# The leaky activation as a maximum, and an earlier start of w_out2's conversion

## The chip, the cores and the metric

One core of one Trainium2 chip. The metric is the device time of one execution in microseconds (us); the kernel before was run three times.

## The reference

Retention attention with a decay per head feeds two gated networks, one behind the other:

```python
ret = scores * Dmat                 # causal, decay gamma ** (i - j), per head
x = (ret @ v)                       # 2304 tokens x 512
y = ((x @ w1) * (x @ w2)) @ w3 @ w_out            # 512 -> 1024 -> 512
h = y @ moe2_w_in                                  # 512 -> 2048
g = np.maximum(h, 0.0) + alpha * np.minimum(h, 0.0)   # alpha: one per column, rand() * 0.3
out = g @ moe2_w_out                               # 2048 -> 512
```

q, k, v, alpha and the result are float32; the weights arrive as float64 and are turned into float32 on the chip.

## The kernel before, in words

Everything is in feature-major tiles of 128 partitions. Every large product runs three times on TensorE (PE), over a high and a low part of each operand: high by high, high by low, low by high. The order on PE, on ScalarE (ACT) and on SyncE (SP, the only queue that issues DMAs) is the order of the code. VectorE (DVE) is ordered by the scheduler; a built program has one fixed order for it too. Semaphores make each engine wait where an operand isn't there.

The stages are attention (to 70 us), a and b and their product (to 279 us), w3 times w_out (to 323 us), y (to 422 us), the **g stage** and the **out stage**. The change touches the last two, and a few tiny instructions early in the attention.

**g stage** (class Group, L871 to L935, loop at L970). The 2304 tokens are three pairs p of blocks of 384 (W), the 2048 columns of h are eight groups j of 256 (m is its half). For one (p, j) a Winograd scheme makes h from seven products of six matmuls, of 384 columns each, 42 in all: p1, p5, p6, p2 of this group and, in between, p7, p4, p3 of the group before (its order on PE is p1, p5, p7 before, p6, p2, p4 before, p3 before). PSUM banks b1, b2, b3 hold the sums. p1 is followed by an ACT copy of b1 to b2 (L909), on which p6 adds; p5 and p6 by ACT copies of their sums into SBUF tiles p5 and u2 (L914, L919). Two of the four tiles of h are ready in PSUM after p2 and p4, and from_psum makes g of them: two Relu on ACT (L894, L895), one scalar_tensor_tensor on DVE (L896). The other two are the sum of a bank and of p5 or u2, after p7 and p3, and from_sum takes three DVE instructions each (L902, L903, L904). p4 writes the bank that p7's from_sum reads, so PE waits for L902. g goes to DRAM (keep, L867) from six SBUF buffers.

**w_out2's conversion** (class Weights, L57 to L136). 16 tiles of 128 x 512 float64 go through four steps: raw is loaded by SP (three buffers); `_first` is two ACT instructions (L93, L94); `_second` four on DVE (L103, L104, L106, L108); `_third` an ACT cast to the high part (L112); `_fourth` a DVE subtraction for the low part (L116). One `tick` does each step once, for pieces one apart, in the order fourth, third, second, first. So the cast of a piece stands on ACT ahead of what the program does next, and waits for L108 of that piece. In pair p = 2, one tick follows each group j from 2 on; the first out steps do the rest.

**out stage** (L1030). 48 steps (j, b): blocks 0 and 1 are done together, j by j, then the others. A step loads g back (load_g, into gr, three buffers), splits it (split_g, one step ahead: an ACT cast to gh, L172, a DVE subtraction to gl, L173) and runs 18 matmuls of 512 columns on three banks. The first matmuls of a step need gh, the third needs gl. The first three load_g are in groups j = 5, 6, 7 of p = 2, split_g(0) in j = 7.

`al` holds alpha in its first 16 columns, and its negative in the next 16 (L863, one DVE instruction that the scheduler puts at 20 us).

Of the kernel before, what the change touches and what calls it, by code (L numbers as in the profile page):

```python
# [11 lines left out]
AF = mybir.ActivationFunctionType  # L12
ALU = mybir.AluOpType
# [11 lines left out]
C2 = DF2 // P  # L25
# [7 lines left out]
def _f32(ap):  # L33
    return ap.bitcast(F32)
# [24 lines left out]
class Weights:  # L59
# [14 lines left out]
        self.pieces, self.raw, self.ab, self.dest = [], {}, {}, {}  # L74
        self.loaded, self.at = 0, [0] * 4

    def add(self, src, dest):

        self.pieces.append((src, dest))

    def load_until(self, n):
        while self.loaded < min(n, len(self.pieces)):
# [26 lines left out]

    def _third(self, i):  # L110
        self.dest[i] = self.pieces[i][1]()
        self.nc.scalar.copy(self.dest[i][0], self.ab[i][0])  # L112

    def _fourth(self, i):
        hi, lo = self.dest.pop(i)
        self.nc.vector.tensor_tensor(out=lo, in0=self.ab.pop(i)[0], in1=_f32(hi), op=ALU.subtract)  # L116

    def tick(self, upto=None):

# [18 lines left out]
def retention_moe_kernel(ctx: ExitStack, tc, qk, kv, w_out1, w3t, w12, w_in, w_out2, alpha, c_row, c_pair, out):  # L138
# [11 lines left out]


    al = const.tile([P, 96], F32, name="al")
    al, neg = al[:, 0:C2], al[:, C2:2 * C2]
    const_r = pool(ctx, "const_r", side="right")
    const_r.tile([P, 120], F32, name="pad")

# [35 lines left out]
    def goes_to(table, key, make):  # L192
        def dest():
            t = make()
            table[key] = t[:, 0], t[:, 1]
            return table[key]
        return dest
# [654 lines left out]
    def wb_tile(c):  # L852
        if c < 8:
            return in_wa(C1 + c, f"wb{c}")
        if c < 14:
            return hold.tile([P, 2, DM], F32R, tag=f"wu{c}", name=f"wb{c}")
        return in_wa(c - 14, f"wb{c}")

    n_in = len(ws.pieces)
    for c in range(C2):  # L860
        ws.add(w_out2[c], goes_to(wbc, c, lambda c=c: wb_tile(c)))

    nc.vector.tensor_scalar(out=neg, in0=al, scalar1=-1.0, scalar2=None, op0=ALU.mult)  # L863

    gd = {}

# [4 lines left out]
    class Group:  # L871
# [16 lines left out]
        def tile(self, tag, bufs=2):  # L888
            return gp.tile([P, W], F32, tag=tag, name=f"{tag}{self.n}", bufs=bufs)

        def from_psum(self, ps, m, t):
            c = 2 * self.j + m
            r, g = self.tile("m"), self.tile("g", 6)
            nc.scalar.activation(r, ps, AF.Relu, scale=-1.0)  # L894
            nc.scalar.activation(g, ps, AF.Relu)  # L895
            nc.vector.scalar_tensor_tensor(out=g, in0=r, scalar=neg[:, c:c + 1], in1=g, op0=ALU.mult, op1=ALU.add)  # L896
            keep(c, 2 * self.p + t, g)

        def from_sum(self, a, b, m, t):
            c = 2 * self.j + m  # L900
            r, g = self.tile("m"), self.tile("g", 6)
            nc.vector.tensor_tensor(out=g, in0=a, in1=b, op=ALU.add)  # L902
            nc.vector.tensor_scalar(out=r, in0=g, scalar1=0.0, scalar2=al[:, c:c + 1], op0=ALU.min, op1=ALU.mult)  # L903
            nc.vector.scalar_tensor_tensor(out=g, in0=g, scalar=0.0, in1=r, op0=ALU.max, op1=ALU.add)  # L904
            keep(c, 2 * self.p + t, g)

        def p1(self):
            self.product(self.b1, "A11", "B11")
# [1 line left out]

        def p5(self):
            self.product(self.b3, "S1", "T1")
            self.p5s = self.tile("p5")
            nc.scalar.copy(self.p5s, self.b3)  # L914

        def p6(self):
            self.product(self.b2, "S2", "T2", False)
            self.u2 = self.tile("u2")
            nc.scalar.copy(self.u2, self.b2)  # L919

        def p2(self):
            self.product(self.b1, "A12", "B21", False)
# [47 lines left out]
    for n, (p, j) in enumerate(groups):  # L970
        last, first = j == C1 - 1 and p + 1 < NP, j == 0 and p > 0
        g = Group(p, j, n)
        flush()
        g.p1()
        g.p5()
        if last:
            some_of(make, 1)
        if before:
            before.p7()
        flush()  # L980
        if first:
            some_of(make, 2)
        g.p6()
        if last:
            some_of(make, 1)
        g.p2()
        if last:
            some_of(make, 1)
        flush()
        if before:  # L990
            before.p4()
            if first:
                some_of(make, 2)
                if p + 1 < NP:
                    x_room(p + 1)
                    for o in range(KT):
                        for t in range(2):
                            nc.sync.dma_start(out=xs_of[p + 1][:, o, t], in_=x2d[2 * (p + 1) + t, o])
                else:
                    pt.close()  # L1000
                    gr = pool(ctx, "gr", side="left", bufs=3, reuse_waits="tile")
                    ghl = pool(ctx, "ghl", side="left", bufs=2, reuse_waits="tile")
            before.p3()
        if j == 5 and p + 1 < NP:
            make = x_operands(p + 1)
        if j in (5, 6):
            some_of(make, 1)
        if p == 0:
            some_of(fetches, 4)
        if p == NP - 1:  # L1010
            if j == 0:
                ws.load_until(n_in + 3)
            if j >= 2:
                ws.tick()
            if j >= 5:
                load_g(j - 5)
            if j == 7:
                split_g(0)
        before = g
# [10 lines left out]
    for n, (j, b) in enumerate(steps):  # L1030
        if ws.at[3] < len(ws.pieces):
            ws.tick()
            ws.until(n_in + 2 * j + 2)
        load_g(n + 3)
        split_g(n + 1)
        if b not in accs:
            accs[b] = [bank((used + i) % 8, f"o{b}_{i}") for i in range(NM)]
# [92 lines left out]
```

## Time and profile before

| | us |
|---|---|
| median of three runs (lowest to highest) | 803.81 (803.64 to 804.98) |
| the profiled execution: span | 801.9 |
| PE busy in it | 787.0 (98%) |
| DVE busy in it | 498.6 (62%) |
| ACT busy in it | 348.9 (44%) |
| g stage, first to last matmul | 422.3 to 599.9 |
| out stage, first to last matmul | 599.9 to 798.4 |

The page gives the profiled execution's span alone, 1.9 us below the median of the runs; what lies around the span isn't on it. Times of rows are counted from the span's start. A row of the timeline has the start, the length of one instruction (or of a group, from its first start to its last end), the engine, the line and operation, out<-in, the shape and the count; in brackets the engine's idle time before it, and who ended it. Instructions of an engine overlap a little, so the distance from start to start (the pitch) is what one costs its engine, and its length is what the next engine waits for. PE's clock stands at its full level in every stretch of the g and out stages.

### The profile page before, as it was taken

What the parts mean: (1) busy time and instruction counts of PE and PEld (TensorE: products, weight loads), DVE (VectorE), ACT (ScalarE), POOL (GpSimd) and SP (SyncE); (2) the same over time, 40 slices, a digit from 0 to 9 for tenths busy, and PEclk for the clock granted to TensorE, in tenths of its full rate; (3) what the DMA queues carried; (4) which work ended last, traced back from release to release, by engine and by line L of the source; (5) the groups of instructions that cost most, each with busy time, mean ns of one, the idle gap of its engine ahead of it and who ended that gap; (6) DMA issues with size and microseconds to landing.
All of it is one profiled execution on the core that took longest, in us unless ns stands there. A gap on an engine that the chain in (4) does not pass through costs nothing.

```text
span 801.9 us, 12688 instructions
## 1 busy us (share of the span) xinstructions
PE 787.0 (98%) x4768; PEld 694.4 (87%) x4768; DVE 498.6 (62%) x895; ACT 348.9 (44%) x648; POOL 0.2 (0%) x4
## 2 busy tenths in 40 slices
PE   7899999999999999999999999999999999999998
PEld 4678888888888988999999999999987888888886
DVE  4895785325477799888833677587899923222232
ACT  3453562231255566656514465465666522222121
POOL 0000000000000000000000000000000000000000
PEclk8999999999999999999999999999999999999999
DMA  9843931561366669899916925225557635344341
GB/s 347 343 159 120 345 150 54 166 247 54 116 201 181 201 201 353 285 400 407 381 46 216 358 100 197 109 98 199 184 194 247 209 99 177 106 132 138 99 136 42
DMA packets 81341, 156.24 MB, mean 195 GB/s; under 512 B 9600, under 2 KB 57728, under 8 KB 81280
## 3 DMA queue, kind: packets, MB, share of 16 engines
q1 hardware_dynamic: 81280, 155.43, 55.6%
q8 instruction: 37, 0.61, 0.3%
q14 instruction: 24, 0.20, 0.1%
HBM read 104.02 MB, written 51.38 MB: 194 GB/s over the span
## 4 chain that ended last, share of the span: by engine, by line
PE 90%; DVE 4%; DMA 2%; issue 1%; ACT 1%; SPq 1%; ACTq 0%; DVEq 0%
PE ps L179 25%; PE o L1045 23%; PE h L884 18%; PE y L817 12%; PE pw L631 5%; PE sc L287 2%; PE o L342 2%; PE o L333 1%; PE st L302 1%; DMA kv<-in_kv_dram 1%; DMA xs<-x2d 1%; DMA gr<-gd 0%; DVE gl L173 0%; DVE g L902 0%; DVE g L896 0%
## 5 line engine op out<-in xcount | busy, mean ns | idle before, releaser
L179 PE MATMUL ps<-xh,w 128*128 128x512 f32 (+1 forms) x640 | 186.0, 372 | 0.6 <-DVE w L116 0.3
L1045 PE MATMUL o<-wb,gh 128*128 128x512 f32 x576 | 177.6, 389 | 1.1 <-ACT gh L172 1.1
L179 PEld LDWEIGHTS ps<-xh,w 128*128 128x128 f32 x640 | 116.0, 188 | 22.3 <-DVE w L116 0.7
L1045 PEld LDWEIGHTS o<-wb,gh 128*128 128x128 f32 x576 | 108.1, 188 | 23.8 <-ACT gh L172 1.5
L179 PE MATMUL ps<-xl,w 128*128 128x512 f32 (+1 forms) x320 | 118.0, 369 | 0.0
L1045 PE MATMUL o<-wb,gl 128*128 128x512 f32 x288 | 112.3, 390 | 0.4 <-DVE gl L173 0.4
L173 DVE TENSOR_TENSOR gl<-gr,gh 128x768 fp32r<-128x768 f32 x48 | 45.9, 957 | 100.1 <-ACT gh L172 100.1
L817 PE MATMUL y<-yab,wp 128*128 128x384 f32 x576 | 100.0, 334 | 0.0
L817 PEld LDWEIGHTS y<-yab,wp 128*128 128x128 f32 x576 | 99.9, 188 | 0.1
L172 ACT CAST gh<-gr 128x768 fp32r<-128x768 f32 x48 | 40.2, 838 | 116.5 <-PE o L1045 112.0
L179 PEld LDWEIGHTS ps<-xl,w 128*128 128x128 f32 x320 | 60.4, 189 | 9.8 <-DVE xl L173 0.3
L1045 PEld LDWEIGHTS o<-wb,gl 128*128 128x128 f32 x288 | 54.1, 188 | 12.5 <-DVE gl L173 1.3
L896 DVE SCALAR_TENSOR_TENSOR g<-m,al,g 128x384 f32<-128x384 f32 x48 | 29.7, 618 | 49.3 <-ACT g L895 47.8
L884 PE MATMUL h<-xT,wv 128*128 128x384 f32 x288 | 54.9, 334 | 1.5 <-DVE g L902 1.5
L884 PE MATMUL h<-xT,wu 128*128 128x384 f32 x288 | 55.0, 335 | 0.5 <-ACT h L909 0.3
L884 PEld LDWEIGHTS h<-xT,wv 128*128 128x128 f32 x288 | 50.3, 188 | 1.8 <-DVE g L902 1.8
L108 DVE CUSTOM_DVE_ANT_0 a<-a,b 128x1024 uint16<-128x1024 uint16 x72 | 49.5, 688 | 3.3
L884 PEld LDWEIGHTS h<-xT,wu 128*128 128x128 f32 x288 | 50.2, 188 | 1.1 <-ACT h L909 0.6
L488 ACT CAST ab<-f 128x512 fp32r<-128x512 f32 (+1 forms) x40 | 23.1, 577 | 63.8 <-DVE f L492 59.4
L492 DVE TENSOR_TENSOR f<-f,ps 128x512 f32<-128x512 f32 (+1 forms) x40 | 25.3, 632 | 30.8 <-PE ps L179 30.6
L103 DVE TENSOR_SCALAR a<-a 128x512 f32<-128x512 f32 x72 | 30.4, 422 | 22.3 <-ACT a L93 21.9
L631 PE MATMUL pw<-wo,w 128*128 128x512 f32 x192 | 43.7, 389 | 0.0
(95 smaller groups left out, 1008.8 us busy)
## 6 DMA issues: line engine op xcount, KB each, us to landing
gd<-g SPq DMA_DIRECT2D x96, 192.0 KB, 1.9
gr<-gd SPq DMA_DIRECT2D x96, 192.0 KB, 2.6
abd<-ab SPq DMA_DIRECT2D x32, 512.0 KB, 4.1
raw<-in_w_out_dram SPq DMA_DIRECT2D x24, 512.0 KB, 3.9
yab<-abd SPq DMA_DIRECT2D x24, 384.0 KB, 8.2
raw<-in_w_dram SPq DMA_DIRECT2D x16, 512.0 KB, 6.9
raw<-in_w3t_dram SPq DMA_DIRECT2D x16, 512.0 KB, 4.1
rawi<-in_w_in_dram SPq DMA_DIRECT2D x16, 512.0 KB, 6.1
```

Source lines behind the costliest of these rows:

```text
L103: nc.vector.tensor_scalar(out=a, in0=a, scalar1=self.LEAST, scalar2=self.MOST, op0=ALU.max, op1=ALU.min)
L108: nc.vector.tensor_tensor(out=a.bitcast(I32), in0=a.bitcast(I32), in1=b, op=ALU.add)
L172: nc.scalar.copy(hi, src)
L173: nc.vector.tensor_tensor(out=lo, in0=src, in1=_f32(hi), op=ALU.subtract)
L179: nc.tensor.matmul(ps, a, bb, start=(n == 0), stop=(n == last))
L488: nc.scalar.copy(t[:, 0], f)
L492: nc.vector.tensor_tensor(out=f, in0=f, in1=pss[1], op=ALU.mult)
L631: nc.tensor.matmul(acc[i], a[:, ic], bb, start=(k == 0 and n == 0), stop=(k == C1 - 1 and n == 2))
L817: nc.tensor.matmul(ys[o], wpc[c][a][:, oc], yab[b, c][:, bb], start=(c == 0 and i == 0), stop=(c == C1 - 1 and i == 2))
L884: nc.tensor.matmul(ps, a[:, x, ks], b[:, y, k], start=(fresh and n == 0), stop=(n == 5), skip_group_check=True)
L896: nc.vector.scalar_tensor_tensor(out=g, in0=r, scalar=neg[:, c:c + 1], in1=g, op0=ALU.mult, op1=ALU.add)
L1045: nc.tensor.matmul(accs[b][i], x[:, m, ic], y, start=(j == 0 and m == 0 and q == 0), stop=(j == C1 - 1 and m == 1 and q == 2))
```

## The change

g is made as the maximum of h and alpha times h. For a column with alpha over 1 that would be a minimum, so a sign sg (1, or -1 where alpha > 1) multiplies h, and the same sign the rows of w_out2. sal is sg times alpha. from_psum becomes one ACT copy scaled by sg and one DVE scalar_tensor_tensor that reads PSUM; from_sum two DVE scalar_tensor_tensor; the copies to p5 and u2 are scaled by sg; the tile m goes. The cast of a tile of w_out2 is scaled by sg, and its low part comes from a scalar_tensor_tensor. In pair p = 2 a tick follows groups 1 and 2, and two ticks follow each group from 3 on; load_g begins at group 3, with four buffers, and keeps four steps ahead.

```diff
     def _third(self, i):
         self.dest[i] = self.pieces[i][1]()
-        self.nc.scalar.copy(self.dest[i][0], self.ab[i][0])
+        sign = self.pieces[i][2]
+        if sign is None:
+            self.nc.scalar.copy(self.dest[i][0], self.ab[i][0])
+        else:
+            self.nc.scalar.activation(self.dest[i][0], self.ab[i][0], AF.Copy, scale=sign)
...
     def _fourth(self, i):
         hi, lo = self.dest.pop(i)
-        self.nc.vector.tensor_tensor(out=lo, in0=self.ab.pop(i)[0], in1=_f32(hi), op=ALU.subtract)
+        sign, a = self.pieces[i][2], self.ab.pop(i)[0]
+        if sign is None:
+            self.nc.vector.tensor_tensor(out=lo, in0=a, in1=_f32(hi), op=ALU.subtract)
+        else:
+            self.nc.vector.scalar_tensor_tensor(out=lo, in0=a, scalar=sign, in1=_f32(hi), op0=ALU.mult,
+                                                op1=ALU.subtract)
...
-    al, neg = al[:, 0:C2], al[:, C2:2 * C2]
+    al, sg, sal = (al[:, n * C2:(n + 1) * C2] for n in range(3))
...
-        ws.add(w_out2[c], goes_to(wbc, c, lambda c=c: wb_tile(c)))
-
-    nc.vector.tensor_scalar(out=neg, in0=al, scalar1=-1.0, scalar2=None, op0=ALU.mult)
+        ws.add(w_out2[c], goes_to(wbc, c, lambda c=c: wb_tile(c)), sg[:, c:c + 1])
+
+    nc.vector.tensor_scalar(out=sg, in0=al, scalar1=1.0, scalar2=-2.0, op0=ALU.is_gt, op1=ALU.mult)
+    nc.vector.tensor_scalar(out=sg, in0=sg, scalar1=1.0, scalar2=None, op0=ALU.add)
+    nc.vector.tensor_tensor(out=sal, in0=sg, in1=al, op=ALU.mult)
...
         def from_psum(self, ps, m, t):
+            c = slice(2 * self.j + m, 2 * self.j + m + 1)
+            g = self.tile("g", 6)
+            nc.scalar.activation(g, ps, AF.Copy, scale=sg[:, c])
+            nc.vector.scalar_tensor_tensor(out=g, in0=ps, scalar=sal[:, c], in1=g, op0=ALU.mult, op1=ALU.max)
+            keep(2 * self.j + m, 2 * self.p + t, g)
+
+        def from_sum(self, a, b, m, t):
+            c = slice(2 * self.j + m, 2 * self.j + m + 1)
+            g = self.tile("g", 6)
+            nc.vector.scalar_tensor_tensor(out=g, in0=a, scalar=sg[:, c], in1=b, op0=ALU.mult, op1=ALU.add)
+            nc.vector.scalar_tensor_tensor(out=g, in0=g, scalar=al[:, c], in1=g, op0=ALU.mult, op1=ALU.max)
+            keep(2 * self.j + m, 2 * self.p + t, g)
+
+        def scaled(self, tag, src, m):
             c = 2 * self.j + m
-            r, g = self.tile("m"), self.tile("g", 6)
-            nc.scalar.activation(r, ps, AF.Relu, scale=-1.0)
-            nc.scalar.activation(g, ps, AF.Relu)
-            nc.vector.scalar_tensor_tensor(out=g, in0=r, scalar=neg[:, c:c + 1], in1=g, op0=ALU.mult, op1=ALU.add)
-            keep(c, 2 * self.p + t, g)
-
-        def from_sum(self, a, b, m, t):
-            c = 2 * self.j + m
-            r, g = self.tile("m"), self.tile("g", 6)
-            nc.vector.tensor_tensor(out=g, in0=a, in1=b, op=ALU.add)
-            nc.vector.tensor_scalar(out=r, in0=g, scalar1=0.0, scalar2=al[:, c:c + 1], op0=ALU.min, op1=ALU.mult)
-            nc.vector.scalar_tensor_tensor(out=g, in0=g, scalar=0.0, in1=r, op0=ALU.max, op1=ALU.add)
-            keep(c, 2 * self.p + t, g)
+            t = self.tile(tag)
+            nc.scalar.activation(t, src, AF.Copy, scale=sg[:, c:c + 1])
+            return t
...
-                    gr = pool(ctx, "gr", side="left", bufs=3, reuse_waits="tile")
+                    gr = pool(ctx, "gr", side="left", bufs=4, reuse_waits="tile")
...
-            if j >= 2:
+            if j >= 1:
                 ws.tick()
-            if j >= 5:
-                load_g(j - 5)
+            if j >= 3:
+                ws.tick()
+            if 3 <= j < 7:
+                load_g(j - 3)
...
-        load_g(n + 3)
+        load_g(n + 4)
```

In the changed kernel the lines of these instructions are L907 (ACT) and L908 (DVE) in from_psum, L914 and L915 in from_sum, L921 in scaled, L116 (the scaled cast) and L124 (its low part) in Weights, L872 to L874 for sg and sal. In both orders below, the first number in a tile's name is the group in the run of 24, or the piece of the conversion (40 is w_out2's first), or the step.

DVE, pair p = 2, from the last instruction of one group's p4 on, in the kernel before; one whole turn is 13 instructions, and L896 of the next group's p2 is the thirteenth:

```order
L896 SCALAR_TENSOR_TENSOR g20_6206<-m20_6205,al_71,g20_6206 128x384
L902 TENSOR_TENSOR g20_6219<-h20_2_6059,u220_6094 128x384
L116 TENSOR_TENSOR wb1_6228<-a41_6053,wb1_6228 128x512
L103 TENSOR_SCALAR a43_6234<-a43_6234 128x512
L903 TENSOR_SCALAR m20_6218<-g20_6219,al_71 128x384
L104 TENSOR_SCALAR a43_6234<-a43_6234 128x512
L904 SCALAR_TENSOR_TENSOR g20_6219<-g20_6219,m20_6218 128x384
L106 SCALAR_TENSOR_TENSOR a43_6234<-raw43_5963,a43_6234 128x512
L902 TENSOR_TENSOR g21_6266<-h21_1_6148,p521_6163 128x384
L108 ISA a43_6234<-a43_6234,b43_6235 128x1024
L903 TENSOR_SCALAR m21_6265<-g21_6266,al_71 128x384
L904 SCALAR_TENSOR_TENSOR g21_6266<-g21_6266,m21_6265 128x384
```

The same place with the change; the four instructions that follow close the turn of 16 (L108 of piece 46, L106 of 47, L908 of group 22's p2, L108 of 47):

```order
L908 SCALAR_TENSOR_TENSOR g20_6086<-h20_1_5934,al_71,g20_6086 128x384
L914 SCALAR_TENSOR_TENSOR g20_6097<-h20_2_5935,al_71,u220_5968 128x384
L124 SCALAR_TENSOR_TENSOR wb4_6105<-a44_6012,al_71,wb4_6105 128x512
L103 TENSOR_SCALAR a46_6111<-a46_6111 128x512
L915 SCALAR_TENSOR_TENSOR g20_6097<-g20_6097,al_71 128x384
L124 SCALAR_TENSOR_TENSOR wb5_6118<-a45_6025,al_71,wb5_6118 128x512
L104 TENSOR_SCALAR a46_6111<-a46_6111 128x512
L914 SCALAR_TENSOR_TENSOR g21_6155<-h21_1_6033,al_71,p521_6048 128x384
L103 TENSOR_SCALAR a47_6124<-a47_6124 128x512
L106 SCALAR_TENSOR_TENSOR a46_6111<-raw46_5917,a46_6111 128x512
L915 SCALAR_TENSOR_TENSOR g21_6155<-g21_6155,al_71 128x384
L104 TENSOR_SCALAR a47_6124<-a47_6124 128x512
```

A turn goes from eight instructions of g and five of the conversion to six and ten.

DVE at the start of the out stage with the change, up to the low part of g that step 1 needs:

```order
L182 TENSOR_TENSOR gl0_6327<-gr0_5930,gh0_6326 128x768
L106 SCALAR_TENSOR_TENSOR a50_6309<-raw50_6115,a50_6309 128x512
L104 TENSOR_SCALAR a51_6322<-a51_6322 128x512
L908 SCALAR_TENSOR_TENSOR g23_6347<-h23_1_6231,al_71,g23_6347 128x384
L914 SCALAR_TENSOR_TENSOR g23_6358<-h23_2_6232,al_71,u223_6265 128x384
L108 ISA a50_6309<-a50_6309,b50_6310 128x1024
L106 SCALAR_TENSOR_TENSOR a51_6322<-raw51_6201,a51_6322 128x512
L915 SCALAR_TENSOR_TENSOR g23_6358<-g23_6358,al_71 128x384
L108 ISA a51_6322<-a51_6322,b51_6323 128x1024
L124 SCALAR_TENSOR_TENSOR wb10_6367<-a50_6309,al_71,wb10_6367 128x512
L103 TENSOR_SCALAR a52_6373<-a52_6373 128x512
L182 TENSOR_TENSOR gl1_6381<-gr1_6029,gh1_6380 128x768
```

Ahead of gl1, DVE has begun pieces up to 52, the thirteenth; in the kernel before, pieces up to 46, the seventh.

DVE early in the attention, with the change (before, one L863 stands in the place of L872 to L874):

```order
L319 TENSOR_TENSOR S_3_276<-S_2_248,per_row 128x128
L872 TENSOR_SCALAR al<-al 128x16
L873 TENSOR_SCALAR al<-al 128x16
L874 TENSOR_TENSOR al<-al 128x16
L300 TENSOR_TENSOR rt_3_254<-sc_3_253,per_pair 128x2x256
L358 TENSOR_TENSOR xs_2_274<-o_2_259,per_pair 128x256
L321 TENSOR_TENSOR S_3_276<-S_3_276,st_3_268 128x128
```

Each of the three needs the one before it. L300, L358 and L321 are L291, L349 and L312 of the kernel before. PE's order is the same in both kernels.

## Rows read from the trace of the kernel before

**Rows 1.** The page, busy time: engine, us (share of the span), instructions.

```profile
PE 787.0 (98%) x4768; PEld 694.4 (87%) x4768; DVE 498.6 (62%) x895; ACT 348.9 (44%) x648; POOL 0.2 (0%) x4
```

**Rows 2.** Timeline of PE, last groups of the g stage and first out steps.

```profile
565.87 1.20 PE L884 MATMUL h<-xB,wv 128*128 128x384 f32 x6
...
594.99 1.21 PE L884 MATMUL h<-xT,wv 128*128 128x384 f32 x6
597.64 1.33 PE L884 MATMUL h<-xT,wv 128*128 128x384 f32 x6 [1.45 <-DVE g L902]
...
599.86 0.63 PE L1045 MATMUL o<-wb,gh 128*128 128x512 f32 x2
...
603.98 0.61 PE L1045 MATMUL o<-wb,gh 128*128 128x512 f32 x2
604.77 0.50 PE L1045 MATMUL o<-wb,gl 128*128 128x512 f32 x1 [0.18 <-DVE gl L173]
...
612.43 0.39 PE L1045 MATMUL o<-wb,gl 128*128 128x512 f32 x1
613.94 0.73 PE L1045 MATMUL o<-wb,gh 128*128 128x512 f32 x2 [1.12 <-ACT gh L172]
614.93 0.50 PE L1045 MATMUL o<-wb,gl 128*128 128x512 f32 x1 [0.26 <-DVE gl L173]
```

**Rows 3.** Timeline of DVE, p = 2: behind the p4 before group 20; a run without idle time.

```profile
565.98 0.62 DVE L896 SCALAR_TENSOR_TENSOR g<-m,al,g 128x384 f32<-128x384 f32 x1 [0.42 <-ACT g L895]
...
587.82 0.62 DVE L896 SCALAR_TENSOR_TENSOR g<-m,al,g 128x384 f32<-128x384 f32 x1 [0.42 <-ACT g L895]
588.36 0.55 DVE L902 TENSOR_TENSOR g<-h,u 128x384 f32<-128x384 f32 x1
588.82 0.68 DVE L116 TENSOR_TENSOR wb<-a,wb 128x512 fp32r<-128x512 f32 x1
589.42 0.42 DVE L103 TENSOR_SCALAR a<-a 128x512 f32<-128x512 f32 x1
589.76 0.42 DVE L903 TENSOR_SCALAR m<-g,al 128x384 f32<-128x384 f32 x1
590.09 0.42 DVE L104 TENSOR_SCALAR a<-a 128x512 uint32<-128x512 uint32 x1
590.43 0.55 DVE L904 SCALAR_TENSOR_TENSOR g<-g,m 128x384 f32<-128x384 f32 x1
590.89 0.69 DVE L106 SCALAR_TENSOR_TENSOR a<-raw,a 128x512 uint32<-128x512 uint32 x1
591.50 0.55 DVE L902 TENSOR_TENSOR g<-h,p 128x384 f32<-128x384 f32 x1
```

**Rows 4.** Timeline of ACT, the two Relu behind the p4 before group 20.

```profile
565.08 0.49 ACT L894 ACTIVATE m<-h 128x384 f32<-128x384 f32 x1 [0.17 <-ACT g L895]
565.46 0.49 ACT L895 ACTIVATE g<-h 128x384 f32<-128x384 f32 x1
```

**Rows 5.** Groups of instructions, DVE: busy us, mean ns | idle before, what ended it.

```profile
L173 DVE TENSOR_TENSOR gl<-gr,gh 128x768 fp32r<-128x768 f32 x48 | 45.9, 957 | 100.1 <-ACT gh L172 100.1
L896 DVE SCALAR_TENSOR_TENSOR g<-m,al,g 128x384 f32<-128x384 f32 x48 | 29.7, 618 | 49.3 <-ACT g L895 47.8 <-DMA gd<-g 1.4
L904 DVE SCALAR_TENSOR_TENSOR g<-g,m 128x384 f32<-128x384 f32 x48 | 26.7, 556 | 1.1
L902 DVE TENSOR_TENSOR g<-h,u 128x384 f32<-128x384 f32 x24 | 13.2, 551 | 0.0
```

**Rows 6.** Timeline of DVE and PE in the attention, around L863.

```profile
20.30 0.17 DVE L863 TENSOR_SCALAR al<-al 128x16 f32<-128x16 f32 x1 [0.76 <-DMA al<-in_alpha_dram]
...
21.32 0.28 DVE L312 TENSOR_TENSOR S<-S,st 128x128 f32<-128x128 f32 x1
...
21.70 0.46 PE L302 MATMUL st<-kv 128*64 128x64 f32 x8 [0.80 <-issue]
```

More of the change, by code (lines that the diff above doesn't have):

```diff
@@ L75, in __init__, with add @@
         self.loaded, self.at = 0, [0] * 4
-    def add(self, src, dest):
-        self.pieces.append((src, dest))
+    def add(self, src, dest, sign=None):
+        self.pieces.append((src, dest, sign))
     def load_until(self, n):
@@ L912, in p5 @@
             self.product(self.b3, "S1", "T1")
-            self.p5s = self.tile("p5")
-            nc.scalar.copy(self.p5s, self.b3)
+            self.p5s = self.scaled("p5", self.b3, 1)
         def p6(self):
             self.product(self.b2, "S2", "T2", False)
-            self.u2 = self.tile("u2")
-            nc.scalar.copy(self.u2, self.b2)
+            self.u2 = self.scaled("u2", self.b2, 0)
         def p2(self):
```

## The prediction

> **What bounds the kernel now.** I read the page's busy times first: PE is busy for 787.0 of 801.9 us, DVE for 62% [rows 1]. So only PE's stalls can be won, and any other engine counts only in a stretch where it becomes slower than PE. PE's timeline around the end of the g stage comes next. Group 20's p1 starts at 565.87 and the last p7 at 594.99 [rows 2]: 168 matmuls of 384 columns in 29.12 us, 0.1733 each, 7.28 us for a group of 42, without a stall. Then come four stalls, each found as the start minus the start before it and the pitch of what lies between (0.1733, and 4.12 us for the 18 matmuls from 599.86 to 603.98, so 0.229 each, in the out stage) [rows 2]: 597.64 - (594.99 + 6 x 0.1733) = 1.61, 604.77 - (603.98 + 0.46) = 0.33, 613.94 - (612.43 + 0.23) = 1.28, 614.93 - (613.94 + 0.46) = 0.53. Their sum, **3.75 us**, is all that stands there to be won.
>
> Then DVE's timeline in the same groups, for what an instruction costs it, start to start [rows 3]: L896, a scalar_tensor_tensor with a scalar per partition, 0.54; L902 and L904 0.46; L116 0.60; L103 0.34; L903 0.33; L104 0.34; L106 0.61; L108, whose next row isn't shown, 0.60 as L116. One turn of group and tick is 2 x 0.54 + 2 x (0.46 + 0.33 + 0.46) for g and 0.34 + 0.34 + 0.61 + 0.60 + 0.60 for a piece, 3.58 + 2.49 = 6.07 us in PE's 7.28. DVE has 1.2 us to spare per group.
>
> **The change part by part.**
>
> *DVE, the g instructions.* Two L896 and six of from_sum become six scalar_tensor_tensor with a scalar per partition. The nearest row is L896; I take 0.54 for each. Six are 3.24 us, 0.34 less than now. The ends: L904's 0.46, as if the per-partition scalar cost nothing, and 0.62, L896's whole length with no overlap [rows 3, 5].
>
> *DVE, the conversion.* L116 becomes L124, a scalar_tensor_tensor with a scalar per partition; L896 is 0.062 longer than L904 [rows 5], and 0.08 in pitch [rows 3], so I take 0.67 (ends 0.60 and 0.75). A piece is then 2.56. From group 3 of p = 2 on there are two pieces per group: 5.12.
>
> *The balance.* A full turn is now 3.24 + 5.12 = **8.36 us against PE's 7.28**: DVE falls 1.08 us behind in every such group. It isn't free to let the conversion wait: its order is fixed, and ACT's too, where the cast of a piece stands ahead of the next group's L909, on which PE's p6 waits, and waits itself for L108. So PE stalls before p6 in the middle of the g stage, where there is none now; then at the last p4, which waits for L914, and at the first out steps.
>
> *How much.* I follow DVE from the last moment at which PE sets its start. That is behind the p4 before group 20: L896 starts at 565.98 there [rows 3]. Its counterpart L908 waits for one ACT instruction in place of two, whose pitch is 0.38 [rows 4], so it can start at 565.60. From it up to gl1, the low part that out step 1 needs, DVE's order holds 85 instructions: 10 L908, 11 L914 and 11 L915 (32 x 0.54 = 17.28), 11 L124 (7.37), 11 L103 and 10 L104 (7.14), 10 L106 (6.10), 10 L108 (6.00) and gl0 (at most its 0.96 [rows 5]). That is 44.85 us, and gl1 takes 0.96: ready at 565.60 + 44.85 + 0.96 = 611.41. PE without a stall would want it at 594.99 + 18 x 0.1733 + 4.12 + 2 x 0.229 = 602.69. PE loses **8.7 us** up to there. Behind it lie 5 DVE instructions up to gl2 (2.9 us with it) and 8 from there to gl3 (4.5 us), with a step of 4.12 us on PE for each: no more stalls. So 8.7 takes the place of 3.75: +5.0.
>
> *ACT.* From_psum loses one of two Relu, which saves ACT 0.76 us a group; the second tick gives it a cast and two instructions more. ACT is 44% busy [rows 1] and waits for DVE in those groups; its time is within the 8.7. That the scaled copies may be longer than plain ones is covered by the same waits.
>
> *The reloads of g and the loads.* Their SP order moves: four load_g are issued two groups earlier. The stall of 1.28 at step 3 waited for gh [rows 2] and is already counted as won. SP holds a second raw load per group that waits for the previous turn's L106, with g's stores behind it; six buffers for g and a turn of 8.4 us cover that, and if they don't, DVE waits and the sum grows. Bank releases move from ACT to DVE's L908, which reads PSUM itself; a bank is used again after two more groups, which hides it.
>
> *sg and sal.* L863 starts at 20.30, when alpha has landed, and L312, behind it on DVE, ends at 21.60, just before PE goes on at 21.70 after 0.80 idle [rows 6]. L312 reads the bank that PE's L302 writes next, so L863 is on the path. Two more such instructions, each waiting for the one before: 2 x (0.17 + 0.04) = **+0.4**, the 0.04 being the step from the L895 that starts at 565.46 and takes 0.49 [rows 4] to L896 at 565.98 [rows 3]. The ends are 0 (another wait ends later) and 0.5.
>
> The sum: +5.0 + 0.4 = +5.4 on the profiled execution's own 801.9 of span, which the runs' median of 803.81 exceeds by what lies around the span. On the median: **809.2 us**, 0.7% slower. A measurement of this kernel tells some 0.2%, 1.6 us, from no change.
>
> [...] Of the 32 scalar_tensor_tensor, 21 read PSUM. The rows show no charge for that: L902 reads PSUM and takes 551 ns, L904 reads SBUF alone and takes 556 [rows 5]. [...] I go by the rows.
>
> **The rivals.**
>
> *The per-partition scalar is cheap* in the new instructions: 0.46 and 0.60. Then DVE's 44.85 shrinks by 32 x 0.08 + 11 x 0.07 = 3.3, and the time is 805.9. L904 speaks for it, L896 against it [rows 3]. With L915, which reads one tensor, at L903's 0.33, 1.4 less still: 804.5.
>
> *DVE keeps up*, and the time ends on the other side. This decides at a turn of 7.28: with pieces of 2.49, six g instructions must cost 0.38 or less each, which only L903's pitch, 0.33, reaches [rows 3]. Then nothing piles up, the early reloads and weights take away 3.75 less a floor of about 0.7 at the last p4 (L914's length and the steps to and from it), and with the 0.4 the time is 801.2. For it: L915 reads one tensor, and L903 does too. Against it: every scalar_tensor_tensor in the rows, L896, L904 and L106, pays the slower pitch.
>
> *More waits than the sum has*: instructions that read PSUM and a scalar at 0.62 (21 x 0.08 = 1.7), or raw tiles that land late behind the held SP queue and stop ACT's L93. Either gives 811 and up. Nothing in the rows shows it; 811.5 is its middle.
>
> *The change doesn't do what it says*: alpha is under 0.3, so the sign is 1 everywhere and changes no value, but its instructions are paid. The earlier start is in DVE's order, so it does happen; no chance of its own.
>
> **How the numbers follow.** The sum as worked out, 807.5 to 811: 0.66. The cheap scalar: 0.12. More waits: 0.10, half of it under 811.8. DVE keeps up, wholly or nearly: 0.12, half of it faster by over 0.2%, half within it. The range 805.0 to 811.8 holds the first, nearly all of the second and half of the third, 0.82. Faster 0.06, same 0.06, slower 0.88.
>
> **What would show it.** In the profile after: DVE busy nearly without idle time from group 20 of 24 to the first out steps; L908, L914 and L915 at about 0.62 in length; a new PE stall at p6 of groups 20 to 23, before a matmul that waits for ACT's L926 (L909 of before), about 0.5 to 1.1 each; ACT's cast L116 waiting for DVE's L108; the stall at the last p4 above 1.61; from step 2 or 3 on no stall. L874 followed by a PE restart near 22.1 in place of 21.70. It is wrong if DVE shows idle time in groups 21 to 23, or if PE reaches the out stage without a stall before the last p4.

## The result, and the profile after

The changed kernel takes **808.72 us** (median of 6, 807.99 to 810.18), the kernel before, run beside it, 804.39 (6, 803.46 to 806.26): a ratio of 1.0053, 95% interval 1.0037 to 1.0070. It is slower by 4.3 us. The profiled execution is the longest of its six, 810.18, with a span of 808.0.

The page, busy time, after:

```profile
PE 788.9 (98%) x4768; PEld 695.0 (86%) x4768; DVE 485.0 (60%) x849; ACT 340.7 (42%) x600; POOL 0.2 (0%) x4
```

Beside [rows 1], both helpers do less: DVE 13.6 us, ACT 8.2. A kernel that gives its helpers less to do is slower, so the totals don't tell it; the stretch does.

The timeline of PE after, from the p1 before the first new stall on (brackets: the idle time before the row, and who ended it):

```profile
566.34 1.20 PE L895 MATMUL h<-xB,wv 128*128 128x384 f32 x6
...
569.98 1.33 PE L895 MATMUL h<-xT,wv 128*128 128x384 f32 x6 [0.36 <-ACT h L926]
...
577.90 1.33 PE L895 MATMUL h<-xT,wv 128*128 128x384 f32 x6 [0.34 <-ACT h L926]
...
586.10 1.31 PE L895 MATMUL h<-xT,wv 128*128 128x384 f32 x6 [0.62 <-ACT h L926]
...
594.32 1.32 PE L895 MATMUL h<-xT,wv 128*128 128x384 f32 x6 [0.67 <-ACT h L926]
...
601.78 1.33 PE L895 MATMUL h<-xT,wv 128*128 128x384 f32 x6 [1.97 <-DVE g L914]
...
605.04 0.50 PE L1062 MATMUL o<-wb,gl 128*128 128x512 f32 x1 [0.42 <-DVE gl L182]
...
610.23 0.73 PE L1062 MATMUL o<-wb,gh 128*128 128x512 f32 x2 [1.27 <-ACT gh L181]
...
611.23 0.50 PE L1062 MATMUL o<-wb,gl 128*128 128x512 f32 x1 [0.27 <-DVE gl L182]
```

Four stalls at p6 of groups 20 to 23 are new; [rows 2] have none there. The p6 of one group follows the last by 7.92, 8.20 and 8.22 us, where a group of matmuls takes 7.28. The last p4, gl of step 0, gh and gl of step 1 follow; step 3's wait of before is gone. From p1 of group 20 to the first matmul with gl1 it is 611.23 - 566.34 = 44.89 us, against the 602.69 - 565.87 = 36.82 that the prediction works out without a stall: 8.1 lost.

DVE's run, by the timeline of DVE after, from L908 behind the p4 before group 20 (in the kernel before, L896 at 565.98 of [rows 3] stands in its place) to gl1:

```profile
566.12 0.62 DVE L908 SCALAR_TENSOR_TENSOR g<-h,al,g 128x384 f32<-128x384 f32 x1 [0.42 <-ACT g L907]
...
610.22 0.95 DVE L182 TENSOR_TENSOR gl<-gr,gh 128x768 fp32r<-128x768 f32 x1
```

The window over this run (columns: stretch, its length, busy time and count of PE, PEld, DVE, ACT, POOL, then the granted clock, the DMA share and GB/s):

```profile
566.12:610.22 44.10, 38.47 (x207) 35.44 (x205) 44.10 (x85) 32.03 (x57) 0.00 (x0) 1.00 0.70 232
```

DVE has no idle time left in it: 44.10 us for the 85 instructions, where 44.85 was worked out.

What was not expected stands on ACT. Its timeline after, from the first new stall backwards:

```profile
565.50 0.58 ACT L907 ACTIVATE g<-h,al 128x384 f32<-128x384 f32 x1 [0.46 <-PE h L895]
565.98 0.71 ACT L116 ACTIVATE wb<-a,al 128x512 fp32r<-128x512 f32 x1
566.59 0.65 ACT L93 ACTIVATE a<-raw 128x512 f32<-128x512 f32 x1
567.15 0.67 ACT L94 ACTIVATE b<-raw 128x512 int32<-128x512 uint16 x1
567.71 0.72 ACT L116 ACTIVATE wb<-a,al 128x512 fp32r<-128x512 f32 x1
568.32 0.67 ACT L93 ACTIVATE a<-raw 128x512 f32<-128x512 f32 x1
568.89 0.67 ACT L94 ACTIVATE b<-raw 128x512 int32<-128x512 uint16 x1
569.46 0.47 ACT L926 COPY h<-h 128x384 f32<-128x384 f32 x1
...
573.43 0.58 ACT L907 ACTIVATE g<-h,al 128x384 f32<-128x384 f32 x1 [0.46 <-PE h L895]
```

No brackets between L907 and L926: in group 20 ACT waits for nobody. Two ticks, six instructions, stand in its queue between the last copy of a p4 and the L926 on which p6 waits. From L907 to the next one is 573.43 - 565.50 = 7.93 us, the 7.92 of PE's p6. So here ACT's queue and PE make a loop longer than PE's 7.28 without DVE: 3.96 us from L907 to L926 (565.50 to 569.46), the rest from there over PE's p6, p2 and p4 to the next L907. Only in groups 22 and 23 does ACT's L93 wait for DVE's L124, 0.16 and 0.21.

Last, the granted clock behind the stalls of step 1, windows of one us after:

```profile
611.00:612.00 1.00, 0.77 (x3) 0.68 (x4) 1.00 (x3) 1.00 (x3) 0.00 (x0) 0.96 0.87 321
612.00:613.00 1.00, 1.00 (x4) 0.70 (x3) 1.00 (x3) 0.65 (x1) 0.00 (x0) 0.50 1.05 390
613.00:614.00 1.00, 1.00 (x4) 0.81 (x3) 1.00 (x3) 0.00 (x0) 0.00 (x0) 0.50 0.12 43
614.00:615.00 1.00, 1.00 (x4) 0.81 (x3) 1.00 (x3) 0.05 (x1) 0.00 (x0) 0.50 0.71 209
615.00:616.00 1.00, 1.00 (x5) 0.78 (x4) 0.96 (x2) 1.00 (x2) 0.00 (x0) 0.83 0.93 341
```

PE is busy in each of them, but from 612 to 615 at a granted clock of 0.50. A pair of matmuls with gh takes 0.85 us from start to start there (612.53 to 613.38) and 0.46 from 615.91 on. By the windows, 0.04 + 3 x 0.50 + 0.17 = 1.7 us, an estimate, are lost to no wait at all. In the profiled execution of before the clock stood at 1.00 in this part of the kernel.

Attention, DVE after, which answers to [rows 6]:

```profile
20.51 0.17 DVE L872 TENSOR_SCALAR al<-al 128x16 f32<-128x16 f32 x1 [0.18 <-DMA al<-in_alpha_dram]
20.71 0.18 DVE L873 TENSOR_SCALAR al<-al 128x16 f32<-128x16 f32 x1
20.93 0.17 DVE L874 TENSOR_TENSOR al<-al 128x16 f32<-128x16 f32 x1
21.02 0.68 DVE L300 TENSOR_TENSOR rt<-sc,per_pair 128x512 f32<-128x512 f32 x1
```

The row behind L863 in the kernel before:

```profile
20.39 0.68 DVE L291 TENSOR_TENSOR rt<-sc,per_pair 128x512 f32<-128x512 f32 x1
```

From the first to L300 it is 0.51, where L863 to L291 was 0.09.

### The profile page after: what moved, and what is told of

It reads as the page before. It is cut to its first block, busy times and chain, and to the rows that moved or that the text cites. A ratio compares the mean times of both kernels' runs of the same rounds, so it can differ in the third digit from the quotient of the medians.

```text
span 808.0 us, 12579 instructions
## 1 busy us (share of the span) xinstructions
PE 788.9 (98%) x4768; PEld 695.0 (86%) x4768; DVE 485.0 (60%) x849; ACT 340.7 (42%) x600; POOL 0.2 (0%) x4
## 4 chain that ended last, share of the span: by engine, by line
PE 90%; DVE 5%; DMA 2%; issue 1%; ACT 1%; SPq 0%; DVEq 0%; ACTq 0%
PE ps L188 25%; PE o L1062 24%; PE h L895 17%; PE y L826 12%; PE pw L640 5%; PE sc L296 2%; PE o L351 2%; PE o L342 1%; DMA kv<-in_kv_dram 1%; PE st L311 1%; DVE wb L124 1%; DVE a L106 1%; DVE a L108 1%; DVE g L914 1%; DMA gd<-g 0%
## 5 line engine op out<-in xcount | busy, mean ns | idle before, releaser
L908 DVE SCALAR_TENSOR_TENSOR g<-h,al,g 128x384 f32<-128x384 f32 x48 | 29.4, 615 | 42.0 <-ACT g L907 39.2
L108 DVE CUSTOM_DVE_ANT_0 a<-a,b 128x1024 uint16<-128x1024 uint16 x72 | 49.5, 688 | 3.1
L103 DVE TENSOR_SCALAR a<-a 128x512 f32<-128x512 f32 x72 | 30.4, 422 | 27.7 <-ACT a L93 27.3
L93 ACT ACTIVATE a<-raw 128x512 f32<-128x512 f32 x56 | 37.5, 669 | 15.0 <-DMA raw<-in_w_dram 7.9
```

Of the source, the lines that this page charges most:

```text
L93: nc.scalar.activation(a, raw.bitcast(F32).rearrange("p (n w) -> p n w", w=2)[:, :, 1], AF.Abs)
L103: nc.vector.tensor_scalar(out=a, in0=a, scalar1=self.LEAST, scalar2=self.MOST, op0=ALU.max, op1=ALU.min)
L108: nc.vector.tensor_tensor(out=a.bitcast(I32), in0=a.bitcast(I32), in1=b, op=ALU.add)
L908: nc.vector.scalar_tensor_tensor(out=g, in0=ps, scalar=sal[:, c], in1=g, op0=ALU.mult, op1=ALU.max)
```

## The experiments

All are timed beside the kernel before; its median was 803.96 beside the first four, 804.11 beside the next four, 803.68 beside the three after that and 804.31 beside the last one. The first four ran on one chip, the next seven on a second, the last on a third. A ratio, with its 95% interval, is to the kernel before of the same group, estimated from all executions, so it isn't quite the quotient of the medians. Profiles are of one execution each.

**The rewrite alone.**

```diff
-            if j >= 1:
-                ws.tick()
-            if j >= 3:
+            if j >= 2:
                 ws.tick()
-            if 3 <= j < 7:
-                load_g(j - 3)
+            if j >= 5:
+                load_g(j - 5)
...
-                    gr = pool(ctx, "gr", side="left", bufs=4, reuse_waits="tile")
+                    gr = pool(ctx, "gr", side="left", bufs=3, reuse_waits="tile")
...
-        load_g(n + 4)
+        load_g(n + 3)
```

> The activation's rewrite with the sign alone: ticks, load_g and gr as in the kernel before. The theory that DVE's queue decides (a turn of group and conversion longer than PE's 7.28 us): the turn is 3.2 + 2.5 = 5.7 us, so no stall at p6 of groups 20 to 23; the stall at the last p4 stays at 1.6 to 2.1, the out steps' at 2 or less, and 0.4 comes from sg and sal: 803.0 to 805.0, not told from before. The theory that the rewrite itself costs (a scaled ACT copy, or PSUM read by DVE): PE stalls all along the g stage, 806 or more.

803.82 us (12 runs), ratio 0.9992 (0.9981 to 1.0004). Making g another way is neutral in time. It isn't the same in the trace: step 3's wait of before, 1.12 for gh [rows 2], is gone, and only 0.26 for gl is left there; against that the last p4 waits 1.82 where it waited 1.45, a stretch at a granted clock of 0.58 and 0.57 follows in this execution (last section), and sg and sal are paid.

**The schedule alone**, on the activation of before, with three buffers for the reloads.

```diff
-            if j >= 2:
+            if j >= 1:
                 ws.tick()
-            if j >= 5:
-                load_g(j - 5)
+            if j >= 3:
+                ws.tick()
+            if 3 <= j < 6:
+                load_g(j - 3)
```

> The earlier ticks and load_g alone, the activation and the cast as in the kernel before, gr with three buffers. DVE's queue decides: a turn is 3.6 + 5.0 = 8.6 us, longer than the change's 8.2, so the p6 stalls of groups 20 to 23 and those behind them come to 0.5 to 1.5 more than with the change: 808.5 to 811. The theory that ACT's order decides (the two ticks ahead of the copy L909): the ACT work behind p4 is 0.1 longer than with the change: 808 to 809.5. The theory that the rewrite costs: within 1.5 us of before.

810.22 us (6), ratio 1.0071 (1.0054 to 1.0089). The timeline of its PE:

```profile
566.27 1.20 PE L884 MATMUL h<-xB,wv 128*128 128x384 f32 x6
...
570.07 1.31 PE L884 MATMUL h<-xT,wv 128*128 128x384 f32 x6 [0.52 <-ACT h L909]
...
603.13 1.33 PE L884 MATMUL h<-xT,wv 128*128 128x384 f32 x6 [2.20 <-DVE g L902]
...
611.91 0.73 PE L1047 MATMUL o<-wb,gh 128*128 128x512 f32 x2 [1.60 <-ACT gh L172]
...
613.20 0.50 PE L1047 MATMUL o<-wb,gl 128*128 128x512 f32 x1 [0.57 <-DVE gl L173]
```

The stalls of the changed kernel are all here, none of them shorter. The loss is the schedule's. The rewrite softens it: up to the first matmul with gl1 it is 613.20 - 566.27 = 46.93 here, 44.89 in the changed kernel. The times don't show it, as the intervals of the two ratios overlap; this execution has no half-speed stretch (a clock of 1.00 in its windows from 560 to 795), the changed kernel's has (0.50 from 612 to 615).

**One tick per group**, from group 1 on, all else as changed.

```diff
             if j >= 1:
                 ws.tick()
-            if j >= 3:
-                ws.tick()
             if 3 <= j < 7:
```

> The change with one tick per group from group 1 on, in place of two from group 3. DVE's queue decides, or ACT's order: both say that the p6 stalls go (turn of 5.7 us on DVE, 2.2 us of ACT work ahead of the copy), and the reloads and weights are still a group further on than before, so the out steps' stalls of 2.1 shrink too: 802.0 to 804.0. The theory that the rewrite costs: 806 or more.

803.05 us (12), ratio 0.9976 (0.9963 to 0.9988): a little faster than before. PE has one stall left from 560 us on:

```profile
598.61 1.33 PE L895 MATMUL h<-xT,wv 128*128 128x384 f32 x6 [1.82 <-DVE g L914]
```

So the second tick is the whole loss. With the earlier start no stall is left in the out steps; that this makes it faster than the rewrite alone isn't shown, as the two ratios' intervals overlap.

**DVE's load lowered**, both ticks kept: the clamp (L103) and the sign bit (L106) are left out for w_out2's tiles.

```diff
     def _second(self, i):
...
+        if self.pieces[i][2] is not None:
+            nc.vector.tensor_scalar(out=ai, in0=ai, scalar1=5, scalar2=2,
+                                    op0=ALU.logical_shift_left, op1=ALU.logical_shift_right)
+            nc.vector.tensor_tensor(out=a.bitcast(I32), in0=a.bitcast(I32), in1=b, op=ALU.add)
+            return
```

> The change with L103 and L106 left out for the 16 tiles of w_out2 (no clamp, no sign bit: another value in out), so DVE's turn is 8.2 - 2 x 0.94 = 6.3 us, under PE's 7.28, while ACT's order and work stay. DVE's queue alone decides: no p6 stalls, 803 to 805. ACT's order is enough: the p6 stalls of groups 20 to 23 stay at 0.5 each (a period of 7.9 us: 3.96 from the cast's predecessor to the copy, 0.52 to p6, 3.45 to the next p4's end), without growing from group to group as they do now (0.52, 0.50, 0.78, 0.83): 805.5 to 807.

805.19 us (12), ratio 1.0009 (0.9998 to 1.0021), between the two ranges that were expected. The timeline of its PE, first and last of four stalls at p6:

```profile
569.22 1.32 PE L900 MATMUL h<-xT,wv 128*128 128x384 f32 x6 [0.36 <-ACT h L931]
...
593.01 1.32 PE L900 MATMUL h<-xT,wv 128*128 128x384 f32 x6 [0.35 <-ACT h L931]
```

DVE is busy 31.6 of the 40 us from 560 on, and still all four stand, 7.93 us apart, with no growth: (593.01 - 569.22) / 3. That is the loop of ACT's queue and PE by itself. The stalls of the out steps are gone; those were DVE's. The last p4 still waits, 1.82.

**The ticks apart**, the same work.

```diff
         g.p2()
         if last:
             some_of(make, 1)
+        if p == NP - 1 and j >= 3:
+            ws.tick()
         flush()
...
             if j >= 1:
                 ws.tick()
-            if j >= 3:
-                ws.tick()
```

> The changed kernel with the two ticks of a group apart: the second one from group 3 of p = 2 on follows p2 in the middle of the group instead of the first tick at its end. DVE's work is the same. ACT-order theory (the stalls at p6 come because two ticks stand on ACT between two copies L926): the four p6 stalls of the changed kernel, 0.5 to 0.8 each, go, and the time falls by 2 to 2.6, to about 806. DVE-load theory (a turn of 8.2 us of DVE work against 7.28 sets the sum, and where ACT's work stands only says where it is paid): the stalls of groups 20 and 21 shrink, those of the last p4 and of gl0, gh1 and gl1 grow by as much, DVE stays without idle time in groups 20 to 23, and the time is 808 to 809, no faster than the changed kernel's 808.7. I expect the second.

807.81 us (11), ratio 1.0042 (1.0029 to 1.0055), just under what DVE's load was to give. It is 0.9 below the changed kernel, but the intervals of the two ratios overlap. PE and ACT, from the timelines of this kernel:

```profile
565.74 1.20 PE L895 MATMUL h<-xB,wv 128*128 128x384 f32 x6
...
593.38 1.32 PE L895 MATMUL h<-xT,wv 128*128 128x384 f32 x6 [1.19 <-ACT h L926]
...
600.71 2.01 PE L895 MATMUL h<-xT,wv 128*128 128x384 f32 x6 [1.85 <-DVE g L914]
...
610.69 0.50 PE L1062 MATMUL o<-wb,gl 128*128 128x512 f32 x1 [0.26 <-DVE gl L182]
```

```profile
588.18 0.72 ACT L116 ACTIVATE wb<-a,al 128x512 fp32r<-128x512 f32 x1 [0.58 <-DVE a L108]
...
591.11 0.73 ACT L116 ACTIVATE wb<-a,al 128x512 fp32r<-128x512 f32 x1 [0.60 <-DVE a L108]
```

The stalls of groups 20 and 21 are gone, group 22 keeps 0.62, group 23 has 1.19. They come now from the cast L116 that waits for DVE's L108, the chain that the prediction drew. Against its expectation, the later stalls didn't grow: the last p4 waits 1.85, gh1 0.96.

So up to gl1 ACT's order costs the changed kernel next to nothing: from p1 of group 20 to the first matmul with gl1 it is 610.69 - 565.74 = 44.95 us here and 44.89 there. DVE stands still once on the way here, 0.40 for a store of g, so 0.4 is the most that ACT's order can hide. What differs is where the half-speed stretch lies, here from 601 to 605; one window of it:

```profile
602.00:603.00 1.00, 1.00 (x5) 1.00 (x4) 1.00 (x4) 0.24 (x1) 0.00 (x0) 0.50 1.04 388
```

It lies ahead of gh1, for which PE has to wait anyway, so its 1.7 us (by the mean clock of 0.66 from 600 to 605, 5 x 0.34) take the place of waits; in the changed kernel the like stretch lies behind gl1 and is paid in full. Behind gl1 the span goes on for 195.2 us here and for 196.8 there.

**Ticks apart and DVE's load lowered**, the two diffs above together.

> The ticks apart as in the run before, and two of the conversion's four DVE instructions left out for w_out2's tiles (the clamp L103 and the sign bit L106, so that part of the conversion isn't done). If ACT's order and DVE's load are all that the double ticks cost: no stall at p6, one stall of some 1.8 at the last p4, none in the out steps, 802.5 to 803.5 as with one tick per group. If the tick's other effects count too (two raw loads per group on SP, four more reloads in the g stage), p6 stalls or a wait for a DMA are left and the time is 805 or more.

803.28 us (12), ratio 0.9982 (0.9968 to 0.9996), one stall, 2.00, at the last p4. With both causes away the second tick costs nothing that these runs tell (803.05 with one tick), so they show no third. The four corners: both causes 808.72, DVE's load alone 807.81, ACT's order alone 805.19, neither 803.28. DVE's load is worth 4.5 alone, ACT's order 1.9 alone, both 5.4; each of these differences can be off by over 1 us. Beside DVE's load ACT's order adds 0.9 or nothing: while PE waits for ACT, DVE works on.

**Out step 0 ahead of the last p4**, on the kernel with one tick.

```diff
-            if j == 7:
+            if j == 6:
                 split_g(0)
...
     before.p7()
     flush()
+    out_step(0)
     before.p4()
     before.p3()
...
-    for n, (j, b) in enumerate(steps):
+    for n in range(1, len(steps)):
+        out_step(n)
```

> One tick per group, and out step 0 moved between the last p7 and the last p4 (split_g(0) one group earlier, so that its operands are there). The 18 matmuls, 4.12 us, cover the wait of p4 for L914. Against one tick alone, 803.05 with the stall at 1.8: the stall goes, 801.2 to 801.8, if a stall of up to 0.4 in step 1 is all that is left. The rival: the wait only moves, as DVE puts gl0, gl1 and the conversion ahead of L914, and the time stays within 0.5 of 803.05. On the clock: some executions with the stall show a mean clock of 0.993 to 0.994, and are some 1.6 us longer than those at 0.995 and above. If the stall is what brings this on, all executions here show 0.995 or more and lie within 1 us of each other; if not, two groups stay.

**799.98 us** (6, 799.74 to 800.14), ratio 0.9940 (0.9921 to 0.9960): 3.1 less than with one tick alone, which is more than the stall itself and under the 801.2 to 801.8 expected. No stall is left in PE's timeline from 545 to 640 us. Every execution shows a mean clock of 0.995 or more, and they lie within 0.4 us.

**Alpha loaded late**, on the kernel with one tick.

```diff
-    nc.sync.dma_start(out=al, in_=alpha)
     load_apart(1, 2, 10)
...
+    nc.sync.dma_start(out=al, in_=alpha)
     x_room(0)
```

> One tick per group, and the load of alpha issued before the last stage ahead of the g stage (where x_room(0) is), so that sg and sal are no longer in the attention. By the prediction's step (0.4 us of L872 to L874 on the path): 802.6 against 803.05 with one tick alone, and PE's wait near 22 us falls from 0.65 or more to 0.2. If the wait for alpha's own landing goes as well (DVE idle 0.2 to 0.9 ahead of L872): 802.0 to 802.5. If another wait ends just behind it: 803.0, as before.

802.48 us (12), ratio 0.9968 (0.9952 to 0.9984), 0.57 below one tick alone, which the two intervals don't tell apart; the trace does. PE's wait near 22 us, 0.65 in the changed kernel, is gone. From PE's L311 at 12.49 to its L351 at 30.69 it is 18.20 us in the changed kernel, 17.29 here (12.10 to 29.39) and 17.85 in the run that follows (11.89 to 29.74). DVE, timeline of this kernel:

```profile
19.67 0.68 DVE L300 TENSOR_TENSOR rt<-sc,per_pair 128x512 f32<-128x512 f32 x1
```

L300 has no wait before it and starts 0.21 behind the L319 ahead of it: the three instructions, and what the wait for alpha put on top, were on the path.

**All three edits together**: the diffs of one tick, of step 0 and of alpha.

> One tick per group, out step 0 ahead of the last p4, and alpha loaded late: the three edits that each gave time, together. The first two gave 799.98; loading alpha late gave 0.57 against one tick alone (802.48 against 803.05). If the gains add: 799.4 (799.0 to 799.8). If something ends just behind the attention's wait: 800.0.

**799.17 us** (6, 798.95 to 799.66), ratio 0.9940 (0.9925 to 0.9955). The gains add: all six executions lie below all six without the late alpha. This beats both kernels, by 0.6% that of before.

**Step 0 ahead of the last p4 in the kernel before**, by the same diff, nothing else.

> The kernel before with out step 0 moved between the last p7 and the last p4 (split_g(0) one group earlier), nothing else. Its stall of 1.61 at the last p4 is covered; the stall of 1.28 with 0.53 behind it at step 3 stays, as its reload of g comes as late as before. If the half-speed stretch of TensorE comes on after the last p4's stall, no execution shows a mean clock of 0.994 or less and the median falls by the 1.61 and by the share of slow-clock executions: 801.5 to 802.3. If the stall at step 3 brings it on as well, two groups of executions stay, about 2 us apart, and the median is 802 to 804.

801.52 us (7, 801.03 to 801.85), ratio 0.9969 (0.9956 to 0.9981). The wait at step 3 stays, as the timeline of its PE shows, and no execution has a mean clock under 0.996:

```profile
607.09 0.73 PE L1039 MATMUL o<-wb,gh 128*128 128x512 f32 x2 [1.11 <-ACT gh L172]
```

**Step 0 ahead of the last p4 in the changed kernel**, by the same diff, both ticks kept.

> The changed kernel with out step 0 moved ahead of the last p4 (split_g(0) one group earlier), both ticks of a group kept. DVE-load theory: what DVE has to finish up to gl1 is the same, so the cover only moves the wait from the last p4 to gh1 and gl1: 807 to 808.7, less than 1.7 gained, and what is gained is the half-speed stretch if that goes. Rival, each stall a loss of its own: the 2.1 us of the last p4 go, 806.0 to 806.6.

809.42 us (6), ratio 1.0066 (1.0050 to 1.0081): nothing is gained. The timeline of its PE:

```profile
594.66 1.31 PE L895 MATMUL h<-xT,wv 128*128 128x384 f32 x6 [1.39 <-ACT h L926]
...
608.78 0.73 PE L1056 MATMUL o<-wb,gh 128*128 128x512 f32 x2 [2.42 <-ACT gh L181]
...
610.32 0.80 PE L1056 MATMUL o<-wb,gl 128*128 128x512 f32 x1 [0.80 <-DVE gl L182]
```

The last p4 no longer waits, and gh1 waits 2.42 in its place. The same edit gives 3.1 us where DVE keeps up and none where it doesn't: the sum of DVE's work up to gl1 sets the time, and a cover for one wait on the way only moves it. The clock still falls behind the new stall, to 0.50 from 610 to 612. The time is 0.7 above the 807 to 808.7 that was expected.

**The activation of before in the best version**: from_psum, from_sum, the copies and the cast as in the kernel before, and one buffer less for the reloads.

```diff
-                    gr = pool(ctx, "gr", side="left", bufs=4, reuse_waits="tile")
+                    gr = pool(ctx, "gr", side="left", bufs=3, reuse_waits="tile")
...
-            if 3 <= j < 7:
+            if 3 <= j < 6:
                 load_g(j - 3)
...
-        load_g(n + 4)
+        load_g(n + 3)
```

> The last combination (799.17) with the activation, the copies and the cast of the kernel before: one tick per group from group 1 on, reloads from group 3, out step 0 ahead of the last p4, alpha late, but g made with two Relu and three-instruction sums, and three buffers for the reloads of g (a fourth has no room beside the tile m). If the rewrite is worth nothing, as it was alone (803.82 against 803.96): 799.0 to 799.5. If its lighter DVE turn or the fourth buffer counts once the other waits are gone: a stall of 0.4 to 1.2 stays at gh or gl of the first out steps, 799.7 to 800.5.

800.70 us (6, 799.50 to 801.46), ratio 0.9949 (0.9934 to 0.9964). The timeline of its PE has one stall:

```profile
607.79 0.50 PE L1039 MATMUL o<-wb,gl 128*128 128x512 f32 x1 [0.54 <-DVE gl L173]
```

It lies 1.5 above the best, more than this stall; but the chip is another, and the intervals of the two ratios overlap, so a difference isn't shown. Whether the DVE turn or the buffer makes the stall can't be told from this run.

## Why the prediction was right, and where not

The forecast was 809.2 with a range of 805.0 to 811.8; 808.72 came. Part of this nearness is luck: the forecast was +5.4 on a kernel before of 803.81, measured is +4.3 on 804.39, and in it is a loss by the clock that the forecast leaves out. By its steps:

- **DVE can't keep up**: right, and the cause: DVE's run without idle time sets what PE loses up to gl1, with the ticks apart as well. The groups of instructions after:

```profile
L915 DVE SCALAR_TENSOR_TENSOR g<-g,al 128x384 f32<-128x384 f32 x48 | 29.5, 616 | 0.8
L908 DVE SCALAR_TENSOR_TENSOR g<-h,al,g 128x384 f32<-128x384 f32 x48 | 29.4, 615 | 42.0 <-ACT g L907 39.2 <-DMA gd<-g 1.4 <-DMA raw<-in_w_out_dram 1.2
...
L124 DVE SCALAR_TENSOR_TENSOR wb<-a,al,wb 128x512 fp32r<-128x512 f32 x16 | 11.9, 744 | 0.0
```

  The new instructions cost 0.53 (taken: 0.54) and L124 0.66 (0.67) from start to start. A turn, L908 at 582.59 to L908 at 590.84, is 8.25 where 8.36 was worked out.
- **8.7 us lost up to gl1**: 8.1 measured; the run was 0.75 shorter than its sum. Against the 3.75 of before that is +4.3 in place of +5.0. The spans of the two profiled executions differ by 6.1: these 4.3, the clock's 1.7, a g stage that starts 0.9 later (423.26 against 422.32, 0.4 of it sg and sal), less 0.5 in the g stage before group 20 (143.08 against 143.55). That is 0.3 too much, which isn't placed. The 0.5 is no gain of the change: the kernel before with step 0 moved, whose code is the same up to there, takes 143.07.
- **No stall behind gl1, step 3's wait won**: right. The next stall behind 611.23 doesn't come.
- **ACT "waits for DVE in those groups; its time is within the 8.7"**: the first half failed, the second held. The stalls at p6 were forecast in place and size (0.5 to 1.1; the distances of 7.92 to 8.22 are 0.64 to 0.94 over 7.28), but from the cast L116 that waits for L108. In groups 20 and 21 it is ACT's own queue, a sum that I never made: from L907 over two ticks to L926 it is 3.96 us, and 3.97 from there to the next L907. In groups 22 and 23 L93 waits for L124 as well. No L116 ahead of a p6 waits for L108 in the changed kernel; with the ticks apart it does. With DVE's load lowered this queue is worth 1.9 us by itself; in the changed kernel it is within the 8.1, as the time up to gl1 is the same with the ticks apart, to 0.4 at the most. A forecast for a lighter DVE made in this way would have missed the 1.9. The 44% of the page hid it: a busy share says nothing of six instructions that stand in a row ahead of the one PE waits for.
- **Step 1 waits for gl1**: it waits first for gh1, 1.27, whose cast stands on ACT behind an L116 that waited 3.88 for L108.
- **sg and sal, +0.4**: right. 0.51 - 0.09 = 0.42 on DVE. On PE, from the L311 at 12.49 to the one at 22.33 it is 9.84, where L302 of before, 12.22 to 21.70, had 9.48: 0.36.
- **The clock**: not in the prediction. In the profiled execution its 1.7 us more than make up for the 0.7 by which the waits fell short, so the number is nearer than its parts.
- **The rivals**: the scalar isn't cheap; DVE keeps up with one tick only; raw tiles aren't late, as ACT's L93 never waits for a DMA from 560 to 612.
- **PSUM or SBUF**: the rows held. L908 reads one of its two tensors from PSUM and takes 615 ns, L915 reads SBUF alone and takes 616: no charge for PSUM here either.

## What to carry to other kernels

When work is moved into a stage, add up one turn of every engine there, and on engines with a fixed order also the queue ahead of the instruction that the bounding engine waits for. Here, with DVE's turn of 8.25 us longer than PE's 7.28, covering the wait at the last p4 moved it to gh1 and gained nothing (809.42 against 808.72); with one tick, where DVE keeps up, other work of PE in front of that wait gained all of it, and more (a stall of 1.82, a gain of 3.1). Where work is to start earlier, add up first whether each engine can do it at that rate: here one tick per group fits (803.05), two don't (808.72).

## What the runs showed of the hardware

In the run with the rewrite alone more is lost at the last p4 than the stall's own length. PE waits 1.82 there, and the windows of its trace go on:

```profile
596.00:598.00 2.00, 0.29 (x2) 0.30 (x3) 2.00 (x6) 0.87 (x2) 0.00 (x0) 1.00 0.32 118
598.00:600.00 2.00, 2.00 (x9) 2.00 (x9) 1.98 (x3) 0.47 (x1) 0.00 (x0) 0.58 0.28 101
600.00:602.00 2.00, 2.00 (x8) 1.86 (x7) 1.17 (x3) 2.00 (x5) 0.00 (x0) 0.57 0.41 125
```

PE is nearly idle for 2 us, then busy for 4 us at a mean granted clock of 0.58 and 0.57: 2 x 0.42 + 2 x 0.43 = 1.7 us more, an estimate. It doesn't follow each time. In the profiled executions with one tick (1.82), with the schedule alone (2.20) and with ticks apart and DVE's load lowered (2.00) the clock stayed at 1.00. Over all runs: of 80 executions of the kernel before, 54 with a mean clock of 0.995 and above have a median of 803.49, 26 at 0.994 and below one of 805.67. The changed kernel has 0.994 or less in all six, and so it has with step 0 moved. The four kernels in which step 0 covers the last p4 and DVE keeps up have it in none of 25. This fits the 3.1 that the edit gave on a stall of 1.8: with one tick alone, six of twelve executions at 0.995 and above have a median of 801.88, six at 0.994 and below one of 803.50, and 799.98 is 1.9 under the first. What decides it from one execution to the next stays open.
